# Moving the first batch's value loads, zero fills, mask products and weight loads to other places in the queues

## The chip, the core and the metric

The kernel runs on one core of a Trainium2 chip. A core has five engines that run side by side, each with its own queue that is worked off in order: TensorE (PE, with its weight loads shown apart as PEld), VectorE (DVE), ScalarE (ACT), GpSimd (POOL) and SyncE (SP). SP, ACT and POOL also issue DMA transfers, which 16 DMA engines carry out. The metric is the device time of one execution in microseconds (us), lower is better.

## The reference

The input is a sliding-window attention over 8 batches of 8 heads, 576 tokens of 64 elements each, followed by a two-layer feed-forward network with a leaky ReLU:

```python
def _attn_ref(q, k, v):                       # each (8, 8, 576, 64)
    scores = scale * np.matmul(q, k.transpose(0, 1, 3, 2))
    mask = np.abs(pos[:, None] - pos[None, :]) <= 32
    scores = np.where(mask, scores, -1000000000.0)
    attn = softmax(scores)
    return np.matmul(attn, v)

def _moe_ref(x, w_in, w_out):                 # x (4608, 512), w_in (512, 2048), w_out (2048, 512)
    h = x @ w_in
    g = np.maximum(0.01 * h, h)
    return g @ w_out
```

All inputs and the output are float32 in the chip's main memory.

## The kernel before

**Tiling.** Heads are taken in pairs (`p`, 0 to 3), so that two heads of 64 elements fill 128 partitions. Each batch is cut into two halves of 288 tokens. A unit of attention is one head pair of one half, numbered `i`: units 0 to 3 are the first half of batch 0, 4 to 7 its second half, 8 to 15 batch 1, and so on. `score(i)` multiplies queries and keys inside the window into a PSUM tile `ps`, ACT takes the exponential into `e` (L305), and a mask product gives `pr` (L309, on POOL). `weighted(i)` multiplies `pr` with a matrix of ones into the row sums `s` (L317 and L318) and with the values into `x` (L325); DVE takes the reciprocal of `s` (L331) and the product into `xT` (L333). There is one `ps`, one `s` and one `x` buffer; `e` and `pr` have two each.

**Feed-forward.** For each half `g` of 288 tokens, `h_tile(g, f)` computes 128 of the 2048 hidden columns (L344, four matmuls over the four head pairs of `xT`), and ACT applies the leaky ReLU into `gT` (L348). `o_tile(j)` computes 128 rows of the output over all 16 hidden tiles (L358), ACT copies it out (L363) and issues the store (L364).

**Preparation of an input.** q and k come in as float32, are cast to bfloat16 (`qb`, `kb`), transposed on PE in pieces of 96 tokens, and copied out of PSUM into `qT` and into `kbd`, which holds the two heads' keys as a block-diagonal matrix. The values are cast straight into the diagonal blocks of `vbd`. So `kbd` and `vbd` must be zero outside the blocks before they are used.

**The order.** The program sets it by hand: each engine works its instructions in the order in which the Python code emits them. Batch 0 is loaded in two parts: part 0 is what units 0 to 3 need, part 1 the rest. All these loads stand on SP's queue (L105 for q and k, L114 for v), pair by pair. POOL builds the mask and casts the keys (`kb`, L215) and some values (L228), DVE casts the queries (`qb`, L215), ACT casts other values (L226). `kbd` of batch 0 is zeroed on DVE (L154, L427), `vbd` on ACT for pairs 0 to 2 (`clear`, L150) and on DVE for pair 3 (L429). The weights come in four quarters each, `w_in`(0) to (3) (512 hidden columns each, four h tiles) and `w_out`(0) to (3), issued from POOL's queue (L419, L423), since they are cast to bfloat16 on the way.

From L425 the first four units are written out. Then h tiles of half 0 alternate with part 1's preparation and units 5 to 7 (`step()`, which emits the next score and this unit's weighted sum). After them come the loads of batch 1: the first is held back by a 4-byte copy from the second quarter of `w_out` into its buffer (L68), so that the weights go first. Behind batch 0's second h group a plan with estimated costs and due times spreads the later batches' attention among the matmuls; the change does not touch it.

Of the kernel before, what the change touches and what calls it, by code (L numbers as in the profile page):

```python
# [10 lines left out]
BF16 = mybir.dt.bfloat16  # L11
AF = mybir.ActivationFunctionType
# [4 lines left out]
def kernel(  # L17
# [83 lines left out]
    def load_qk0(p, h):  # L101
        for t, src, part in ((qf[0, p], q, PART_Q[h]), (kf[0, p], k, PART_K[h])):
            t0, run = part
            c0, c1 = columns(part)
            nc.sync.dma_start(  # L105
                out=t[:, :, c0 * D:c1 * D],
                in_=src[0, 2 * p:2 * p + 2, t0:t0 + 96 * run].rearrange(
                    "a (p c) d -> p a (c d)", c=run),
            )

    def load_v0(p, h):
        n0, n1 = PART_V[h]
        for a in range(2):
            nc.sync.dma_start(  # L114
                out=vf[0, p][64 * a:64 * a + 64, n0:n1],
                in_=v[0, 2 * p + a, 64 * n0:64 * n1].rearrange("(c p) d -> p c d", p=64),
            )

    for p in range(NPAIR + 1):
        if p < NPAIR:  # L120
            load_qk0(p, 0)
        if p > 0:
            load_v0(p - 1, 0)
    for p in range(NPAIR):
        load_qk0(p, 1)
        load_v0(p, 1)
# [15 lines left out]

    kbd = [const.tile([128, NPAIR, NB, 128], BF16, name=f"kbd{i}") for i in range(2)]
    vbd = [const.tile([128, NPAIR, NB, 128], BF16, name=f"vbd{i}") for i in range(2)]
    zero = const.tile([128, 1], BF16)
    nc.vector.memset(zero, 0.0)

    def clear(t, p):
        flat = t[:, p].rearrange("p n j -> p (n j)")
        nc.scalar.activation(  # L150
            out=flat, in_=zero.to_broadcast([128, NB * 128]), func=AF.Copy,
        )

    nc.vector.memset(kbd[0][:, 0:2], 0.0)  # L154
    for p in range(3):
        clear(vbd[0], p)

# [50 lines left out]
    def cast_qk0(p, h):  # L210
        for eng, src, dst, part in (
            (nc.vector, qf, qb, PART_Q[h]), (nc.gpsimd, kf, kb, PART_K[h]),
        ):
            c0, c1 = columns(part)
            eng.tensor_copy(  # L215
                out=dst[:, p, c0:c1],
                in_=src[0, p][:, :, c0 * D:c1 * D].rearrange("p a (c d) -> p c a d", d=D),
            )
# [11 lines left out]
    def transposes0(p, h):  # L230

        if 0 not in qT:
            qT[0] = attn.tile([128, NPAIR, S], BF16, name="qT")
        for src, part in ((qb, PART_Q[h]), (kb, PART_K[h])):
            t0, run = part
            c0, c1 = columns(part)
            tp = mmps.tile([128, run, 96], BF16, name="tp0", tag="mm")
            for c in range(run):
                nc.tensor.transpose(
                    tp[:, c], src[:, p, c0 + c].rearrange("p a d -> p (a d)"), ident[0:96, 0:96],  # L240
                )
            if src is qb:
                nc.scalar.activation(
                    out=qT[0][:, p, t0:t0 + 96 * run].rearrange("p (i c) -> p i c", c=run),
                    in_=tp.rearrange("p c i -> p i c"), func=AF.Copy,
                )
            else:
                for a in range(2):
                    r = slice(64 * a, 64 * a + 64)
                    nc.scalar.activation(  # L250
                        out=kbd[0][r, p, t0 // 64:t0 // 64 + 96 * run // 64, r].rearrange(
                            "p n (i c) -> p n i c", c=run),
                        in_=tp[r].rearrange("p c (n i) -> p n i c", i=64 // run), func=AF.Copy,
                    )

    def transposes(b, first=False):

# [36 lines left out]
    def score(i):  # L294
        b, hf, p = where(i)
        ps = scps.tile([128, 1024], FP32, name="ps")
        c0 = 512 - HALF
        for blk, q0, n in WIN[hf]:
            nc.tensor.matmul(  # L299
                ps[:, c0:c0 + n], kbd[b % 2][:, p, blk],  # L300
                qT[b][:, p, q0:q0 + n], start=True, stop=True,
            )
            c0 += n
        e = attn.tile([128, NCOL], BF16, name="e")
        nc.scalar.activation(  # L305
            out=e, in_=ps[:, 512 - HALF:512 - HALF + NCOL], func=AF.Exp, scale=scale,
        )
        pr = attn.tile([128, NCOL], BF16, name="pr")
        nc.gpsimd.tensor_mul(pr, e, mask[hf])  # L309
        probs[i] = pr  # L310

    def weighted(i):
        b, hf, p = where(i)
        pr = probs.pop(i)
        x = xps.tile([128, HALF], FP32, name="x")
        s = xps.tile([128, HALF], FP32, name="s")
        nc.tensor.matmul(s, ones_bd, pr[:, 0:HALF], start=True, stop=False, skip_group_check=True)  # L317
        nc.tensor.matmul(  # L318
            s[:, ODD[hf]:ODD[hf] + NCOL - HALF], ones_bd, pr[:, HALF:NCOL],
            start=False, stop=True, skip_group_check=True,  # L320
        )
        c0 = 0
        for n_, (blk, q0, n) in enumerate(WIN[hf]):
            a = q0 - HALF * hf
            nc.tensor.matmul(  # L325
                x[:, a:a + n], vbd[b % 2][:, p, blk, :], pr[:, c0:c0 + n],
                start=(n_ == 0), stop=(n_ == len(WIN[hf]) - 1), skip_group_check=True,
            )
            c0 += n
        r = attn.tile([128, HALF], FP32, name="r")  # L330
        nc.vector.reciprocal(r, s)  # L331
        t0 = (b * S + hf * HALF) % RING
        nc.vector.tensor_mul(xT[:, p, t0:t0 + HALF], x, r)  # L333
# [87 lines left out]
    def load_w_out(i):  # L421
        c = slice(4 * i, 4 * i + 4)
        nc.gpsimd.dma_start(out=w_out_bf[:, c, :], in_=w_out_r[:, c, :])  # L423

    cast_qk0(0, 0)  # L425
    make_mask(0)
    nc.vector.memset(kbd[0][:, 2:4], 0.0)  # L427
    cast_qk0(1, 0)
    nc.vector.memset(vbd[0][:, 3], 0.0)  # L429
    transposes0(0, 0)  # L430
    transposes0(1, 0)
    cast_v0(0, 0)
    cast_qk0(2, 0)
    score(0)
    transposes0(2, 0)
    score(1)
    cast_v0(1, 0, on_act=True)
    cast_qk0(3, 0)
    weighted(0)
    load_w_in(0)  # L440
    transposes0(3, 0)
    score(2)
    cast_v0(2, 0, on_act=True)
    weighted(1)
    load_w_in(1)
    score(3)
    cast_v0(3, 0, on_act=True)
    make_mask(1)
    load_w_in(2)
    weighted(2)  # L450
    cast_qk0(0, 1)
    load_w_in(3)
    weighted(3)
    state["done"] = NPAIR
    transposes0(0, 1)
    score(4)
    cast_v0(0, 1)


    for f in range(FFC):  # L460
        h_tile(0, f)
        if f % 2 == 1:
            i = (f - 1) // 2
            if i < 3:
                cast_qk0(i + 1, 1)
                cast_v0(i + 1, 1)
                transposes0(i + 1, 1)
            if 1 <= i < 5:
                step()
            if i >= 4:  # L470
                load_w_out(i - 4)

    for p in range(NPAIR):
        load_qk(1, p, w_out_bf[0:1, 4, 0:2] if p == 0 else None)
# [95 lines left out]
```

The softmax here doesn't subtract the row's maximum and nothing guards it: scores larger than these inputs give would overflow.

## Time and profile before

| | |
|---|---|
| median of 6 runs | 361.0 us (360.26 to 362.88) |
| the profiled execution | 360.11 us |
| its span in the profile | 358.4 us |
| PE busy | 327.9 us, 91% of the span |
| PE busy from 0 to 10, 10 to 20, 20 to 30 us | 3.80, 5.83, 8.10 us |
| DVE, ACT, POOL busy | 186.8, 209.5, 177.0 us |
| the DMA engines, from 0 to 10, 10 to 20, 20 to 30 us | share 0.69, 0.89, 1.19 |
| first ACT copy of a transposed query (L243) | starts at 5.48 us |
| exp of units 0, 1, 2, 3, 4 (L305) | start at 8.06, 10.38, 14.44, 16.07, 22.23 us |
| first h tile (L344) | starts at 21.93 us |
| mask products 6 and 7 (L309) | 34.24 to 36.62 us |
| landing of the four quarters of `w_out` | 5.9 us at least, 12.9 at most, after the issue |
| batch 1's first load | issued at 50.01 us |

Times in the profile count from the start of the span. A line of the timeline names the start, the duration, the engine, the line of the kernel, what is written from what, and in brackets how long the engine stood idle before and what ended that. A line of the chain of waits has the start, the duration and what the chain passed through at that time. The DMA share is the mean busy share of the 16 DMA engines; overlapping packets can bring it above 1.

### The profile page before, as it was taken

What the parts mean: (1) busy time and instruction counts of PE and PEld (TensorE: products, weight loads), DVE (VectorE), ACT (ScalarE), POOL (GpSimd) and SP (SyncE); (2) the same over time, 40 slices, a digit from 0 to 9 for tenths busy, and PEclk for the clock granted to TensorE, in tenths of its full rate; (3) what the DMA queues carried; (4) which work ended last, traced back from release to release, by engine and by line L of the source; (5) the groups of instructions that cost most, each with busy time, mean ns of one, the idle gap of its engine ahead of it and who ended that gap; (6) DMA issues with size and microseconds to landing.
All of it is one profiled execution on the core that took longest, in us unless ns stands there. A gap on an engine that the chain in (4) does not pass through costs nothing.

```text
span 358.4 us, 6953 instructions
## 1 busy us (share of the span) xinstructions
PE 327.9 (91%) x2730; PEld 221.8 (62%) x2752; DVE 186.8 (52%) x204; ACT 209.5 (58%) x450; POOL 177.0 (49%) x217
## 2 busy tenths in 40 slices
PE   3668897689989999999999999999999999999995
PEld 1446654458566685757585676758585666667652
DVE  5655503595635554666654654655563665655200
ACT  8736555458375483838474574838383665646441
POOL 7774933637765454665445553655553554222000
PEclk9999999899999999999999999999999999999999
DMA  6894799979786532634343523544320101010101
GB/s 178 164 224 67 117 202 258 232 193 214 174 194 155 186 101 65 174 116 128 97 124 112 183 68 111 148 133 110 81 62 31 59 2 60 1 60 0 60 10 78
DMA packets 62434, 42.39 MB, mean 118 GB/s; under 512 B 39874, under 2 KB 57794, under 8 KB 62402
## 3 DMA queue, kind: packets, MB, share of 16 engines
q1 hardware_dynamic: 52994, 28.32, 33.2%
q0 software_dynamic: 4224, 4.19, 7.2%
q10 hardware_dynamic: 5184, 9.44, 7.1%
q8 instruction: 21, 0.34, 0.4%
q14 instruction: 11, 0.09, 0.1%
HBM read 36.70 MB, written 9.44 MB: 129 GB/s over the span
## 4 chain that ended last, share of the span: by engine, by line
PE 72%; DMA 8%; ACT 7%; POOL 4%; issue 3%; DVE 2%; SPq 1%; ACTq 1%; POOLq 0%; DVEq 0%
PE mm L358 32%; PE mm L344 28%; PE x L325 3%; PE tp L266 3%; PE ps L299 3%; POOL pr L309 2%; DMA w_out_bf<-in_moe_w_out_dram 2%; DMA vf<-in_v_dram 2%; ACT o_sb L363 2%; PE s L317 2%; ACT e L305 1%; DMA qf<-in_q_dram 1%; PE s L318 1%; DMA qf<-w_out_bf 1%; ACT gT L348 1%
## 5 line engine op out<-in xcount | busy, mean ns | idle before, releaser
L331 DVE RECIPROCAL r<-s 128x288 f32<-128x288 f32 x64 | 125.3, 1958 | 94.8 <-PE s L318 94.6
L309 POOL TENSOR_TENSOR pr<-e,mask 128x544 bf16<-128x544 bf16 x64 | 77.6, 1213 | 136.4 <-ACT e L305 134.5
L344 PE MATMUL mm<-xT,w_in_bf 128*128 128x288 bf16 x1024 | 137.4, 290 | 1.5 <-ACT gT L348 1.5
L358 PE MATMUL mm<-w_out_bf,gT 128*128 128x512 bf16 x554 | 129.5, 381 | 1.2
L344 PEld LDWEIGHTS <-w_in_bf 128*128 128x128 bf16 x1024 | 99.2, 99 | 28.3 <-issue 3.2
L348 ACT ACTIVATE gT<-mm 128x288 bf16<-128x288 f32 x256 | 102.2, 412 | 23.6 <-PE mm L344 9.3
L358 PEld LDWEIGHTS <-gT 128*128 128x128 bf16 x576 | 55.3, 98 | 60.0 <-issue 0.6
L363 ACT ACTIVATE o_sb<-mm 128x512 f32<-128x512 f32 x36 | 21.5, 597 | 85.7 <-PE mm L358 85.7
L305 ACT ACTIVATE e<-ps 128x544 bf16<-128x544 f32 x64 | 39.8, 622 | 17.7 <-PE ps L299 9.1
L283 DVE COPY kbd<-kT 64x576 bf16<-64x576 bf16 x56 | 24.8, 444 | 23.8 <-ACT kT L280 23.4
L207 POOL CAST vbd<-vf 64x576 bf16<-64x576 f32 x52 | 34.4, 661 | 1.7
L333 DVE TENSOR_TENSOR xT<-x,r 128x288 bf16<-128x288 f32 x64 | 29.3, 458 | 6.7
L299 PE MATMUL ps<-qT,kbd 128*128 128x128 bf16 (+2 forms) x320 | 27.4, 218 | 2.0 <-ACT e L305 1.2
L197 POOL CAST kb<-kf 96x768 bf16<-96x768 f32 x28 | 23.1, 824 | 12.1 <-DMA kf<-in_k_dram 12.1
L325 PE MATMUL x<-pr,vbd 128*128 128x128 bf16 (+2 forms) x320 | 27.2, 218 | 0.7 <-DVE xT L333 0.5
L299 PEld LDWEIGHTS <-kbd 128*128 128x128 bf16 x320 | 20.8, 101 | 10.0 <-DVE kbd L283 1.3
L317 PE MATMUL s<-pr,ones_bd 128*128 128x288 bf16 x64 | 19.1, 299 | 7.7 <-POOL pr L309 4.8
L325 PEld LDWEIGHTS <-vbd 128*128 128x128 bf16 x320 | 21.8, 102 | 4.9 <-issue 2.1
L274 ACT ACTIVATE qT<-tp 128x576 bf16<-128x576 bf16 x28 | 18.1, 648 | 6.4 <-PE tp L266 5.7
L280 ACT ACTIVATE kT<-tp 128x576 bf16<-128x576 bf16 x28 | 18.2, 650 | 3.0 <-PE x L325 1.4
L197 POOL CAST qb<-qf 96x768 bf16<-96x768 f32 x24 | 19.7, 820 | 0.0
L318 PE MATMUL s<-pr,ones_bd 128*128 128x256 bf16 x64 | 18.3, 286 | 0.0
(43 smaller groups left out, 123.9 us busy)
## 6 DMA issues: line engine op xcount, KB each, us to landing
out_dram<-o_sb ACTq DMA_DIRECT2D x36, 256.0 KB, 2.4
qf<-in_q_dram SPq DMA_DIRECT2D x28, 288.0 KB, 3.3
kf<-in_k_dram SPq DMA_DIRECT2D x28, 288.0 KB, 3.9
vf<-in_v_dram SPq DMA_DIRECT2D x56, 144.0 KB, 3.3
w_in_bf<-in_moe_w_in_dram POOLq DMA_DIRECT2D x4, 512.0 KB, 8.3
w_out_bf<-in_moe_w_out_dram POOLq DMA_DIRECT2D x4, 512.0 KB, 9.7
qf<-in_q_dram SPq DMA_DIRECT2D x8, 144.0 KB, 3.0
kf<-in_k_dram SPq DMA_DIRECT2D x4, 192.0 KB, 3.2
```

Of the source, the lines that this page charges most:

```text
L197: eng.tensor_copy(out=dst[:, p], in_=src[b, p].rearrange("p a (c d) -> p c a d", d=D),)
L207: nc.gpsimd.tensor_copy(out=vbd[b % 2][r, p, :, r], in_=vf[b, p][r])
L299: nc.tensor.matmul(ps[:, c0:c0 + n], kbd[b % 2][:, p, blk], qT[b][:, p, q0:q0 + n], start=True, stop=True,)
L305: nc.scalar.activation(out=e, in_=ps[:, 512 - HALF:512 - HALF + NCOL], func=AF.Exp, scale=scale,)
L309: nc.gpsimd.tensor_mul(pr, e, mask[hf])
L325: nc.tensor.matmul(x[:, a:a + n], vbd[b % 2][:, p, blk, :], pr[:, c0:c0 + n], start=(n_ == 0), stop=(n_ == len(WIN[hf]) - 1), skip_group_c ...
L331: nc.vector.reciprocal(r, s)
L333: nc.vector.tensor_mul(xT[:, p, t0:t0 + HALF], x, r)
L344: nc.tensor.matmul(h[:, 0:HALF], w_in_bf[:, c, ts(f, 128)], xT[:, c, ds(t0, HALF)], start=(c == 0), stop=(c == DMC - 1),)
L348: nc.scalar.activation(out=gT[:, f, ds(t0, HALF)], in_=h[:, 0:HALF], func=AF.Prelu, alpha=0.01,)
L358: nc.tensor.matmul(o, gT[:, f, ds(128 * j % RING, 128)], w_out_bf[:, f, :], start=(f == 0), stop=(f == FFC - 1),)
L363: nc.scalar.activation(out=o_sb, in_=o, func=AF.Copy)
```

## The change

Batch 0 alone is touched; from batch 1's loads on the program is the same. In words:

- Part 0's values of pairs 0 and 1 (four transfers) are issued on ACT's queue, ahead of its activation table load. SP issues q and k of all pairs, with the values of pairs 2 and 3 behind theirs.
- The three fills of `vbd` on ACT and their `zero` tile are gone. DVE fills `vbd` of all four pairs, two behind the cast of q(1) and two behind that of q(2).
- The mask products of units 0 and 1 run on DVE.
- `transposes0` becomes a generator that yields after the query and after the key, so that `score(0)` stands between the two for pair 1.
- `w_in`(2) and (3) and `w_out`(0) move behind casts of part 1 on POOL; the casts of pair 1's part 1 move ahead of the h tiles; and the steps of units 4 to 7 stand behind h tiles 3, 6, 9 and 12 instead of 3, 5, 7 and 9. `w_out`(1) to (3) stay behind the last mask product of batch 0 on POOL.

```diff
-    def load_v0(p, h):
+    def load_v0(p, h, eng=nc.sync):
...
-            nc.sync.dma_start(
+            eng.dma_start(
...
-    for p in range(NPAIR + 1):
-        if p < NPAIR:
-            load_qk0(p, 0)
-        if p > 0:
-            load_v0(p - 1, 0)
+    for p in range(NPAIR):
+        load_qk0(p, 0)
+        if p >= 2:
+            load_v0(p, 0)
+    for p in range(2):
+        load_v0(p, 0, nc.scalar)
...
-    zero = const.tile([128, 1], BF16)
-    nc.vector.memset(zero, 0.0)
-
-    def clear(t, p):
-        flat = t[:, p].rearrange("p n j -> p (n j)")
-        nc.scalar.activation(
-            out=flat, in_=zero.to_broadcast([128, NB * 128]), func=AF.Copy,
-        )
-
     nc.vector.memset(kbd[0][:, 0:2], 0.0)
-    for p in range(3):
-        clear(vbd[0], p)
...
-        nc.gpsimd.tensor_mul(pr, e, mask[hf])
+        (nc.vector if i < 2 else nc.gpsimd).tensor_mul(pr, e, mask[hf])
...
+    t0 = {(p, h): transposes0(p, h) for p in range(NPAIR) for h in range(2)}
+
+    def t_pair(p, h):
+        next(t0[p, h])
+        next(t0[p, h])
+
     cast_qk0(0, 0)
     make_mask(0)
     nc.vector.memset(kbd[0][:, 2:4], 0.0)
     cast_qk0(1, 0)
-    nc.vector.memset(vbd[0][:, 3], 0.0)
-    transposes0(0, 0)
-    transposes0(1, 0)
+    for p in range(2):
+        nc.vector.memset(vbd[0][:, p], 0.0)
+    t_pair(0, 0)
+    next(t0[1, 0])
+    score(0)
+    next(t0[1, 0])
     cast_v0(0, 0)
     cast_qk0(2, 0)
-    score(0)
-    transposes0(2, 0)
+    for p in range(2, 4):
+        nc.vector.memset(vbd[0][:, p], 0.0)
+    t_pair(2, 0)
     score(1)
     cast_v0(1, 0, on_act=True)
     cast_qk0(3, 0)
+    load_w_in(0)
     weighted(0)
-    load_w_in(0)
-    transposes0(3, 0)
+    t_pair(3, 0)
     score(2)
     cast_v0(2, 0, on_act=True)
     weighted(1)
     load_w_in(1)
     score(3)
     cast_v0(3, 0, on_act=True)
+    weighted(2)
     make_mask(1)
-    load_w_in(2)
-    weighted(2)
     cast_qk0(0, 1)
-    load_w_in(3)
     weighted(3)
     state["done"] = NPAIR
-    transposes0(0, 1)
+    t_pair(0, 1)
     score(4)
     cast_v0(0, 1)
+    cast_qk0(1, 1)
+    cast_v0(1, 1)

     for f in range(FFC):
         h_tile(0, f)
-        if f % 2 == 1:
-            i = (f - 1) // 2
-            if i < 3:
-                cast_qk0(i + 1, 1)
-                cast_v0(i + 1, 1)
-                transposes0(i + 1, 1)
-            if 1 <= i < 5:
-                step()
-            if i >= 4:
-                load_w_out(i - 4)
+        if f == 1:
+            cast_qk0(2, 1)
+            load_w_in(2)
+            t_pair(1, 1)
+        if f == 3:
+            step()
+            cast_v0(2, 1)
+            cast_qk0(3, 1)
+            load_w_in(3)
+            t_pair(2, 1)
+        if f == 6:
+            step()
+            cast_v0(3, 1)
+            load_w_out(0)
+            t_pair(3, 1)
+        if f == 9:
+            step()
+            load_w_out(1)
+        if f == 12:
+            step()
+            load_w_out(2)
+            load_w_out(3)
```

More of the change, by code (lines that the diff above doesn't have):

```diff
@@ L246, in transposes0 @@
                 )
+                yield
             else:
@@ L254, in transposes0 @@
                     )
+                yield
     def transposes(b, first=False):
```

## The prediction

> **What bounds the kernel now.** I read the stages view first, then the chain of waits, then the timeline of the first 50 us, then the landing times of the weights. From 80 us to the end TensorE is busy 269.8 of 278 us, and the change touches nothing there. So the question is when that run can begin. The stages view (us, then busy time and instructions of PE, weight loads, DVE, ACT and POOL, granted clock, DMA share, GB/s) shows the start:
>
> ```profile
> 20.00:30.00 10.00, 8.10 (x54) 5.68 (x52) 4.14 (x6) 5.61 (x15) 5.24 (x12) 1.00 1.19 205
> 30.00:38.00 8.00, 5.47 (x53) 3.77 (x51) 6.37 (x6) 4.38 (x11) 5.91 (x8) 1.00 0.02 3
> 38.00:50.00 12.00, 11.79 (x97) 9.24 (x99) 2.81 (x3) 8.88 (x22) 9.66 (x11) 1.00 1.08 173
> 50.00:64.00 14.00, 10.58 (x79) 5.39 (x80) 4.82 (x10) 5.75 (x10) 4.12 (x6) 1.00 1.04 241
> ```
>
> The reader is to see that the DMA engines do next to nothing from 30 to 38 us, and that PE has 3.4 us of idle time from 50 to 64 while they work at 241 GB/s. The chain of waits (start, duration, what) says why:
>
> ```profile
> 33.48 0.63 ACT e L305
> 34.11 0.02 issue
> 34.13 0.02 POOLq L309
> 34.15 0.10 issue
> 34.24 2.38 POOL pr L309 x2
> 36.62 0.74 POOL w_out_bf L423
> 37.37 8.31 DMA w_out_bf<-in_moe_w_out_dram
> 45.67 0.02 SPq L68
> 45.70 0.05 issue
> 45.74 4.24 DMA qf<-w_out_bf
> ...
> 50.92 5.15 DMA qf<-in_q_dram
> 56.09 7.57 DMA vf<-in_v_dram
> ```
>
> Batch 1's loads are held by a 4-byte copy out of the second quarter of `w_out`. That quarter is issued at 37.37, behind mask products 6 and 7 on POOL, and lands at 45.68. The copy takes 4.24, and then q, k and v of batch 1 pass at the engines' rate until 63.66, when the first values allow PE to go on. **The time of the end is therefore set by when `w_out`(1) lands**; the 18 us behind it move as one piece.
>
> What sets mask product 7 goes back to the first heads. On the timeline, DVE:
>
> ```profile
> 10.68 1.96 DVE L331 RECIPROCAL r<-s 128x288 f32<-128x288 f32 x1 [0.55 <-PE s L318]
> ...
> 14.34 1.96 DVE L331 RECIPROCAL r<-s 128x288 f32<-128x288 f32 x1 [1.13 <-PE s L318]
> ...
> 17.05 1.96 DVE L331 RECIPROCAL r<-s 128x288 f32<-128x288 f32 x1 [0.19 <-PE s L318]
> ...
> 19.95 1.94 DVE L331 RECIPROCAL r<-s 128x288 f32<-128x288 f32 x1
> ```
>
> There is one sum buffer, so each reciprocal must end before the next sums start: 2.7 us per head pair at best (17.05 less 14.34). Score 4 and the first h tile stand behind these on PE.
>
> **The change, part by part.** Times below are walked down the five queues in their new order with the rows' durations; the same walk through the old order gives exp 4 ending at 22.84 and product 7 ending at 36.54, where the trace has 22.85 and 36.62.
>
> *ACT's fills leave, four value loads come.* The three fills keep ACT until its first copy at 5.48. Four loads at SP's 0.60 to 0.71 for such a load run from 0.8 to 3.4, the table load (1.28) to 4.7. The first transposes end at 4.4, so the first copy starts at 4.7, 0.8 sooner.
>
> *SP loses four issues ahead of pairs 2 and 3.* q(2) goes out at 2.7 instead of 4.12, k(3) at 5.7 instead of 7.22, the second part at 7.5 instead of 10.35. Landing takes 2.8 to 3.4 us on every load before 10 us, so SP's issue is the limit there. Four value loads more in the first 3 us must cost something: nothing at the least, and at most 1.0 on k(1) (320 KB at the 250 GB/s of that time is 1.3 us, part of it behind k(1)). I take 0.5, the middle, and 0.3 on k(0). The second part's earlier landing buys nothing, because its first cast (19.49) stands on DVE behind the third xT.
>
> *Exp 0.* Key cast at 4.4, transposes to 5.57, two kbd copies (0.97) to 6.6, query copy (0.41), scores by 7.3: exp 0 ends at 7.97 against 8.68. Gain 0.7.
>
> *DVE takes three more fills (0.54 each) and two mask products.* No row shows the product on DVE. The bf16 copy of 64x576 (0.444) bounds it below, the f32 tensor product of 288 columns scaled to 544 (0.458 x 544/288 = 0.87) above. I take 0.50, near the copy, which has the same type and length. Here the change adds a wait: DVE stands for exp 0, and behind it are cast q(2), two fills, product 1, cast q(3) and the first reciprocal. Product 0 ends at 8.5, q(2) is cast at 8.98 instead of 7.86, the pair's copies on ACT end at 10.8, and exp 1 at 11.45 instead of 11.00. Product 1, then cast q(3) (0.5): **the first reciprocal starts at 12.46 instead of 10.68**. From there the 2.7 cadence holds (before, the second one waited for POOL's product until 14.34): 15.16, 17.86 and, behind cast q(0,1), 20.78, against 19.95. Exp 4 ends at 23.69 against 22.85. So the early stage loses 0.84.
>
> *POOL after product 4.* Before, products 5 to 7 waited for ACT and all weights but `w_out` were out by 20.9. Now: product 4 to 24.95, values of pair 0 (0.84), keys 1 (0.40), values 1 (0.84), keys 2 (0.40), `w_in`(2) issued at 27.3 instead of 19.0, product 5 when exp 5 ends (29.7 to 30.9), values 2 and keys 3, `w_in`(3) at 32.05, product 6 at 33.8 (exp 6) to 35.0, values 3, `w_out`(0) at 35.8, product 7 to 37.8, `w_out`(1) at 37.75, against 37.37: 0.4 later. Exp 6 stands behind h tiles 4 to 6. Two tiles took 2.13 at 21.9 and 1.14 at 33.1, with granted clock 1.00 both times; the pace doubled between 31.4 and 32.2. I let it double at 31.1, the start of the idle stretch; all three tiles at the slow pace would cost 0.5 more, all at the fast one 0.9 less. The Trainium skill (TensorE: Matmul & The Clock Gate, Part 1) says that the clock opens after a busy free-running window of about 3.4 us, which would put it anywhere from 29.6 to 33 here and my sum from -1.5 to -0.5.
>
> *The landing.* The first of the four `w_out` quarters landed 5.9 after its issue, the second 3.2 after the first. Now `w_out`(0) has 1.95 us of lead: it lands at 41.7, and `w_out`(1) 3.2 later at 44.9 if the queue stays full, or 5.9 after its own issue at 43.65. I take 44.7, nearer to the first, since the lead is shorter than a quarter's 3.2. Against 45.68 that is 1.0 sooner. So what the late POOL queue loses (0.4) comes back through the head start of `w_out`(0).
>
> *Cover.* `w_in`(2) is costed at nothing because PE reaches h tile 8 only at 34.2 and it lands at 33.2 to 33.8 (5.9, as a lone transfer, to 6.5, as `w_in`(0)). `w_in`(3) lands at 38.1, where PE stands for it about 1 us; then PE ends batch 0's second h group at 49.3 against 49.45. POOL beside DVE's two products is costed at nothing: its key cast 2 ends at 8.25 and cast q(2), which PE needs too, only at 8.98. The Trainium skill (SBUF — State Buffer, Who interferes with whom) has a rule against this move: a DVE operation with two SBUF inputs and a GpSimd operation that reads SBUF block each other for a whole instruction. By it product 0 starts 0.25 later, when POOL's cast ends, and the sum would be -0.75.
>
> **Sum.** -1.0 on a profiled execution of 360.11 (span 358.4 and 1.7 around it). The median of the runs shown is 361.0, 0.9 above that execution, and I carry the difference over: 360.0. A difference under 0.3%, 1.1 us, is about what a measurement here cannot tell from no change.
>
> **The rivals.**
> - *The DVE queue eats it all.* Product at 0.87, k(1) and its followers 1 us later instead of 0.5: the product counts twice ahead of the first reciprocal, +0.75, and the landings +0.5, all passed to product 7 unless POOL absorbs it. `w_out`(1) at 45.5 to 46: about 361.0. For it: reciprocals have no slack after the first. Against: TensorE and POOL waits downstream absorb parts.
> - *Slower: h tile 8 waits for `w_in`(2).* Product 7 stands behind h tiles 8 and 9 on PE, so a late landing holds `w_out`(1). In the profile `w_in` took 6.5, 7.5, 9.2 and 10.7 us to land. From 6.9 (34.2) on it delays product 7; at 9.1 the gain is gone; at 10.7 h tile 8 starts at 38.0, product 7 ends at 41.3, `w_out`(1) lands at 47.2: +1.5, 362.5. For it: the landings shown. Against: the long ones had the loads of q, k, v and another quarter beside them, and by 27 us these are done.
> - *More: the pace of PE doubles early and `w_out` does not queue.* Product 7 ends at 36.9 and `w_out`(1) lands 5.9 behind its issue, 42.8 to 43.5: -2.2 to -2.9, 358.5. For it: SP's loads end sooner. Against: POOL's own casts already fill the time between products 6 and 7.
>
> **How the numbers follow.** Forecast (-1.7 to -0.3, that is 359.3 to 360.7) 0.40, of which 0.25 lies beyond 0.3%; more 0.17; eaten 0.22; slower 0.21. Faster 0.25 + 0.17 = 0.42; same 0.15 + 0.22 = 0.37; slower 0.21. The range reaches from the bound of "more" at 358.4 to 362.4, just below the slow case's price, and leaves about 0.08 below it and 0.11 above.
>
> **What would show it.** Right: ACT's first copy near 4.7; first reciprocal near 12.5 and the fourth near 20.8; exp 4 end near 23.7; `w_out`(1) issued near 37.8, landing within 7.5 us; the 4-byte copy starting near 44.8; PE free of waits on `w_in` before h tile 12. Wrong: PE standing at h tile 8; mask products on DVE over 0.9; loads before 5 us landing in over 4.5; the 4-byte copy taking other than about 4.2 us; or a stage behind 64 us that does not follow the landing.

## The result, and the profile after

The changed kernel takes 359.04 us (median of 34 runs, 356.69 to 361.54) beside 360.65 us for the kernel before (69 runs in all). The ratio is 0.9953 with a 95% interval of 0.9940 to 0.9965: **1.7 us faster** by the ratio (1.6 by the medians), where 1.0 us was forecast. The profiled execution of the changed kernel took 357.59 us (span 355.9); that of before 360.11 (span 358.4).

The stages view of the changed kernel (stretch, length, then busy time and instructions of PE, weight loads, DVE, ACT and POOL, granted clock, DMA share, GB/s):

```profile
20.00:30.00 10.00, 7.86 (x49) 5.33 (x50) 4.44 (x8) 4.65 (x12) 4.22 (x8) 1.00 0.41 74
30.00:38.00 8.00, 7.46 (x70) 5.51 (x67) 7.07 (x6) 6.13 (x17) 6.83 (x10) 1.00 0.83 132
38.00:50.00 12.00, 11.40 (x91) 8.76 (x93) 2.95 (x4) 8.21 (x20) 10.47 (x12) 1.00 1.09 173
50.00:64.00 14.00, 9.79 (x78) 5.11 (x77) 4.82 (x10) 6.92 (x12) 5.28 (x7) 1.00 1.03 276
```

The transfers have moved as the edit says: the stretch from 30 to 38 us, in which the DMA engines carried 3 GB/s, now carries 132, and the one before it 74 in place of 205. But look at the last line: from 50 to 64 us the DMA engines move 276 GB/s in place of 241, at the same share of busy time (1.03 and 1.04). Nothing in the edit is about those loads.

The chain of waits of the changed kernel (start, duration, what) shows the same thing from the other side:

```profile
34.13 1.21 POOL pr L301
...
36.13 0.49 POOL w_out_bf L415
...
36.96 1.16 POOL pr L301
38.12 7.90 DMA w_out_bf<-in_moe_w_out_dram
...
46.04 0.05 issue
46.09 3.58 DMA qf<-w_out_bf
...
49.69 0.33 SPq L70
...
53.04 7.88 DMA kf<-in_k_dram
...
63.28 1.22 POOL pr L301
```

Product 7 ends later than before, `w_out`(1) is issued later (38.12 for 37.37) and lands later: the 4-byte copy behind it starts at 46.09, 0.35 us after that of before. Yet batch 1's first load starts 0.32 us sooner (49.69 for 50.01), since the copy took 3.58 for 4.24, and product 8 starts 1.25 us sooner (63.28 for 64.53). From the first load of batch 1 to product 8 it is 13.59 us where it was 14.52. So **the prediction's earlier landing did not come, and the gain arose behind it**, in a stage that was said to move as one piece.

The queue of DVE in the changed kernel, from its timeline (start, duration, operation; the bracket is idle time before it):

```profile
8.67 0.45 DVE L301 TENSOR_TENSOR pr<-e,mask 128x544 bf16<-128x544 bf16 x1 [1.42 <-ACT e L297]
...
12.08 0.44 DVE L301 TENSOR_TENSOR pr<-e,mask 128x544 bf16<-128x544 bf16 x1 [1.28 <-ACT e L297]
...
12.90 1.95 DVE L323 RECIPROCAL r<-s 128x288 f32<-128x288 f32 x1
...
15.55 1.96 DVE L323 RECIPROCAL r<-s 128x288 f32<-128x288 f32 x1
...
18.23 1.96 DVE L323 RECIPROCAL r<-s 128x288 f32<-128x288 f32 x1 [0.17 <-PE s L310]
...
21.13 1.94 DVE L323 RECIPROCAL r<-s 128x288 f32<-128x288 f32 x1
```

The products are cheap on DVE, the wait for exp 0 and exp 1 stands ahead of them as predicted, and all four reciprocals are late: the first by 2.2 us, the fourth by 1.2.

A second thing moved with it. In the trace of before the granted clock shows a half-pace stretch just behind the end of batch 1's wait; the changed kernel's profiled execution has none. The stage of 65 to 70 us, before:

```profile
65.00:70.00 5.00, 4.16 (x28) 2.49 (x29) 2.42 (x2) 2.48 (x5) 3.21 (x4) 0.66 1.22 214
```

and after:

```profile
65.00:70.00 5.00, 4.89 (x46) 2.85 (x43) 4.45 (x5) 2.41 (x4) 3.38 (x4) 1.00 1.02 271
```

28 matmuls at a mean clock of 0.66 against 46 at full clock. Here the stretch lasts from 65.38 to 68.80 us, 3.4 us at 0.50, which is 1.7 us of pace. The mean clock of a run tells roughly how many such stretches it had: 0.995 (358.4 x 0.005 = 1.8 us) goes with one, about 0.990 with two. Of the 80 runs of before that stand beside the experiments, 11 had a clock of 1.000; of the changed kernel's, 12 of 34.

### The profile page after: what moved, and what is told of

It reads as the page before. It is cut to its first block, busy times and chain, and to the rows that moved or that the text cites. A ratio compares the mean times of both kernels' runs of the same rounds, so it can differ in the third digit from the quotient of the medians.

```text
span 355.9 us, 6950 instructions
## 1 busy us (share of the span) xinstructions
PE 326.1 (92%) x2730; PEld 221.0 (62%) x2752; DVE 189.1 (53%) x208; ACT 206.4 (58%) x447; POOL 174.9 (49%) x215
## 4 chain that ended last, share of the span: by engine, by line
PE 71%; ACT 7%; DMA 6%; issue 4%; POOL 4%; DVE 4%; ACTq 1%; SPq 1%; POOLq 0%; DVEq 0%
PE mm L350 31%; PE mm L336 28%; PE x L317 3%; PE tp L258 3%; PE ps L291 3%; DVE r L323 3%; DMA w_out_bf<-in_moe_w_out_dram 2%; DMA kf<-in_k_dram 2%; ACT o_sb L355 2%; PE s L309 2%; POOL pr L301 2%; PE s L310 1%; ACT e L297 1%; ACT gT L340 1%; ACTq L356 1%
## 5 line engine op out<-in xcount | busy, mean ns | idle before, releaser
L301 POOL TENSOR_TENSOR pr<-e,mask 128x544 bf16<-128x544 bf16 x62 | 75.2, 1213 | 136.6 <-ACT e L297 133.1
L336 PEld LDWEIGHTS <-w_in_bf 128*128 128x128 bf16 x1024 | 99.1, 99 | 30.0 <-issue 3.9
L297 ACT ACTIVATE e<-ps 128x544 bf16<-128x544 f32 x64 | 39.8, 622 | 18.1 <-PE ps L291 9.3
L275 DVE COPY kbd<-kT 64x576 bf16<-64x576 bf16 x56 | 24.8, 443 | 22.4 <-ACT kT L272 22.0
```

The lines of the kernel that those rows point to most:

```text
L297: nc.scalar.activation(out=e, in_=ps[:, 512 - HALF:512 - HALF + NCOL], func=AF.Exp, scale=scale,)
L301: (nc.vector if i < 2 else nc.gpsimd).tensor_mul(pr, e, mask[hf])
L336: nc.tensor.matmul(h[:, 0:HALF], w_in_bf[:, c, ts(f, 128)], xT[:, c, ds(t0, HALF)], start=(c == 0), stop=(c == DMC - 1),)
```

## The experiments

Two parts of the change could be taken apart: the **start** (first values from ACT, fills and two products on DVE) and the **second part** (order of the weights and of the casts). A third difference lies in the addresses. The constant column `zero`, which the change drops, is 2 bytes wide, but it takes 32 bytes of each partition, and every tile allocated behind it lies 32 bytes lower once it is gone, the masks too. The load destinations `qf`, `kf`, `vf`, both weights, `xT` and `gT` begin 32 bytes past a multiple of 256 bytes before, and at one after. All kernels, and how many bytes past a multiple of 256 the load destinations lie (a ratio is of runs on the same chip, so it can differ by some tenths of a microsecond from the medians):

| kernel | start | second part | bytes past | median us | ratio to before (95%) |
|---|---|---|---|---|---|
| before | before | before | 32 | 360.65 | 1 |
| after | change | change | 0 | 359.04 | 0.9953 (0.9940 to 0.9965) |
| `early_only` | change | before | 0 | 360.32 | 0.9993 (0.9970 to 1.0017) |
| `late_only` | before | change | 32 | 358.66 | 0.9938 (0.9915 to 0.9961) |
| `no_lead` | change | change, `w_out`(0) later | 0 | 360.57 | 0.9990 (0.9972 to 1.0009) |
| `w_out_first` | before | before, `w_out`(0), (1) ahead of product 6 | 32 | 356.83 | 0.9874 (0.9845 to 0.9903) |
| `aligned` | before | before | 64 | 360.65 | 1.0001 (0.9976 to 1.0026) |
| `aligned_512` | before | before | 0 | 358.96 | 0.9937 (0.9915 to 0.9959) |
| `after_shifted` | change | change | 32 | 361.08 | 0.9998 (0.9976 to 1.0021) |
| `v_on_sp` | change, values on SP | change | 0 | 357.07 | 0.9889 (0.9861 to 0.9917) |
| `products_on_pool` | change, products on POOL | change | 0 | 361.05 | 1.0010 (0.9992 to 1.0029) |
| `v_sp_w_out` | change, values on SP | change, `w_out`(0), (1) ahead of product 6 | 0 | 357.42 | 0.9903 (0.9874 to 0.9932) |
| `best` | before | change, `w_out`(0), (1) ahead of product 6 | 64 | 356.23 | 0.9875 (0.9843 to 0.9906) |
| `best_loads` | before | as `best` | 0 (loads alone) | 356.90 | 0.9877 (0.9847 to 0.9907) |

### The two parts, each alone

`early_only` keeps the change up to `weighted`(1) and has the order of before from there on:

```diff
-    weighted(2)
     make_mask(1)
+    load_w_in(2)
+    weighted(2)
     cast_qk0(0, 1)
+    load_w_in(3)
...
+        if f % 2 == 1:
+            i = (f - 1) // 2
+            if i < 3:
+                cast_qk0(i + 1, 1)
+                cast_v0(i + 1, 1)
+                t_pair(i + 1, 1)
+            if 1 <= i < 5:
+                step()
+            if i >= 4:
+                load_w_out(i - 4)
```

> The change's first part alone (values issued from ACT, fills and the first two products on DVE, new order of the first units); weights and second part in the order of before. My theory: the first part costs time. Exp 4 ended at 24.03 us in the changed kernel and 22.85 in before, and nothing after it wins that back when the weights stand as before: product 7 ends at 37.8 to 38.1, w_out(1) lands near 47, batch 1's first load goes out near 51.3, and the run is 1.0 to 1.5 us slower than before. Rival (the gain comes from the shorter start on ACT and SP): faster than before by 1 us or more, like the whole change. Rival (the gain is only the half-pace window of PE at 65 us, which comes less often in the changed kernel): within 0.5 us of before.

`late_only` is the other half: the start of before, and the change from `weighted`(2) on.

> The change's second part alone (weights between the casts of the second part, casts of pair 1 earlier, steps behind h tiles 3, 6, 9 and 12); the start as before. My theory: this part holds the whole gain and more, because exp 4 ends at 22.85 as before: product 7 ends near 36.9, w_out(1) lands near 44.1 against 45.68, and the run is 1.0 to 2.0 us faster than before, so 0 to 1 us faster than the whole change (which measured 1.7 us faster). Rival (the gain comes from the start): within 0.5 us of before. Rival (h tile 8 waits for w_in(2)): slower than before, with PE standing at h tile 8 near 33 us.

Measured: `early_only` 360.32 us, `late_only` 358.66. In `early_only` exp 4 starts at 23.85 (22.23 before), `w_out`(1) is issued at 38.99 and batch 1's loads start at 51.55, 1.54 later than before; yet the time is that of before. In `late_only` exp 4 starts at 22.19, `w_out`(1) goes out at 37.15, and the copy behind it starts at 44.98, 0.76 sooner than before, and batch 1's loads at 48.60, 1.41 sooner. So the second part alone is worth 2.0 us, at least as much as the whole change (the intervals of the two ratios overlap). That `early_only` costs nothing, with all its stations over 1 us late, was the first sign of a gain that neither part explains; here too batch 1's loads go faster (14.2 us from the first load to product 8, for 14.5), while in `late_only`, which keeps the column `zero`, they are slower (15.4).

### What the head start of the first quarter is worth

`no_lead` issues `w_out`(0) directly ahead of `w_out`(1), behind product 7:

```diff
             cast_v0(3, 1)
-            load_w_out(0)
             t_pair(3, 1)
         if f == 9:
             step()
+            load_w_out(0)
             load_w_out(1)
```

> The whole change, but w_out(0) is issued behind the last mask product, right ahead of w_out(1). My theory: the head start of w_out(0) is what paid for the late product 7. Without it w_out(0) is issued near 38.1 and w_out(1) lands 8 to 9 us later, near 47, against 46.1 in the changed kernel's profile: 0.9 to 1.9 us slower than the whole change, near before or up to 1 us slower. Rival (the head start does nothing, since w_out(1) landed 7.95 us after its issue with it): the same time as the whole change.

Measured: 360.57 us, 1.5 more than the changed kernel. `w_out`(1) is issued at 38.79 and the copy starts at 47.27, 8.5 us later, where it takes 7.97 with the head start. The prediction's view that the lead makes up for the late POOL queue holds in its sign: 1.2 us of the copy's start, 0.7 of it by the later issue and 0.5 by the longer landing. One caution goes with all such readings of single profiles: the changed kernel, `early_only` and `no_lead` are the same program at the same place up to score 3, and yet exp 1 starts at 11.42, 11.87 and 12.15 us.

`w_out_first` is the kernel before with both first quarters moved ahead of mask product 6 on POOL, and nothing else:

```diff
                 cast_v0(i + 1, 1)
+                if i == 2:
+                    load_w_out(0)
+                    load_w_out(1)
...
-            if i >= 4:
+            if i >= 6:
                 load_w_out(i - 4)
```

> The kernel before, with w_out(0) and w_out(1) issued ahead of mask product 6 instead of behind product 7; nothing else. POOL stood idle there from 32.2 to 34.2 us. My theory that the end follows the landing of w_out(1) one for one: issue of w_out(1) near 33.0 instead of 37.37, landing near 41.3 instead of 45.68, batch 1's first load near 45.5 instead of 50.01, and the time 3 to 4 us lower, until PE takes over as the limit (it stood idle 3.4 us between 50 and 64 us, and lost about 1.7 us to the half pace at 66 us). Rival (the end hangs on something else, such as PE or the rate of the loads): less than 1 us faster.

Measured: 356.83 us, 3.8 less than before. From its timeline, of SP and of POOL:

```profile
41.99 0.72 SPq L68 DMA_DIRECT2D qf<-w_out_bf  x1
46.16 0.34 SPq L70 DMA_DIRECT2D qf<-in_q_dram  x1
...
62.30 1.21 POOL L309 TENSOR_TENSOR pr<-e,mask 128x544 bf16<-128x544 bf16 x1 [0.81 <-ACT e L305]
```

`w_out`(0) and (1) are issued from 32.79 on, the copy starts at 41.99 in place of 45.74, batch 1's first load at 46.16 in place of 50.01. Of 3.75 us at the landing and 3.85 at the loads, product 8 gets 2.2 (62.30), and the time 3.8. The gate that the prediction read from the chain of waits is a right one: moving it moves the time. But the stage behind it stretches, from 14.5 to 16.1 us between the first load and product 8, so the near equality of 3.75 and 3.8 is no proof of one for one; where the other 1.6 us of the time arise was not traced.

### Where the tiles lie

`aligned` and `aligned_512` are the kernel before with a wider `zero`; no instruction is added, removed or moved.

```diff
-    zero = const.tile([128, 1], BF16)
-    nc.vector.memset(zero, 0.0)
+    zero = const.tile([128, 32], BF16)
+    nc.vector.memset(zero[:, 0:1], 0.0)
...
-            out=flat, in_=zero.to_broadcast([128, NB * 128]), func=AF.Copy,
+            out=flat, in_=zero[:, 0:1].to_broadcast([128, NB * 128]), func=AF.Copy,
```

> The kernel before with its constant column `zero` 64 bytes wide in place of 2: every tile behind it, the destinations of all loads among them, lies 32 bytes further on, at multiples of 64 bytes as in the changed kernel (the 2-byte column takes 32 bytes); no instruction is added, removed or moved. Theory 'address': the packets of 256 bytes that bring batch 1, 27.2 ns each in the trace of before and 18.1 in the changed kernel's, take 18 to 19.5 here; from the first load of batch 1 to mask product 8 it is 13.6 to 14.2 us in place of 14.5, so product 8 starts 0.3 to 0.9 us sooner, and the time is 359.7 to 360.3 us beside 360.65. Rival 'start' (the packets are faster for what else the change did at the start): 26 to 27.5 ns, nothing moves, 360.4 to 360.9.

(`aligned_512`: `[128, 256]` in place of `[128, 32]`.)

> The kernel before with its constant column 512 bytes wide: every tile behind it lies at the same place within 512 bytes as in the changed kernel (the 64-byte column left them 64 bytes off). Theory 'address, in 256 or 512 bytes': the 256-byte packets of the stretch that the product stage of batch 1 loads in take 18 to 19 ns in place of 24.6 (the 64-byte column gave 22.0), product 8 starts 0.4 to 0.9 us sooner, and the time is 359.2 to 360.1. Rival 'not the address of the tiles' (the order of the first loads or their queue): 22 to 25 ns, 360.4 to 360.9.

`after_shifted` gives the changed kernel the 32 bytes back (and one small fill on DVE):

```diff
+    unused = const.tile([128, 1], BF16)
+    nc.vector.memset(unused, 0.0)
     nc.vector.memset(kbd[0][:, 0:2], 0.0)
```

> The changed kernel with an unused 2-byte constant where `zero` was: all tiles behind it are 32 bytes off a multiple of 64 again; one memset of some 0.05 us on DVE is added before 1 us. Theory 'address': the 256-byte packets take 25 to 27.5 ns, mask product 8 starts 0.3 to 0.9 us later after the first load of batch 1, and the time is 359.3 to 360.2 us, so that a good part of the 1.7 us gained was the address. Rival 'start': 18 to 19 ns, 358.8 to 359.3.

The DMA view of 59 to 111 us in four kernels: the queue of SP's loads (packets, MB, share of 16 engines' time) and the loads of the values (issues, KB each, median us to landing). Before:

```profile
q1 hardware_dynamic: 18125, 9.09, 86.1%
...
vf<-in_v_dram SPq DMA_DIRECT2D x21, 144.0 KB, 4.7
```

Before with the 512-byte column (`aligned_512`):

```profile
q1 hardware_dynamic: 18098, 9.07, 67.7%
...
vf<-in_v_dram SPq DMA_DIRECT2D x21, 144.0 KB, 3.1
```

The changed kernel:

```profile
q1 hardware_dynamic: 18429, 9.52, 72.7%
...
vf<-in_v_dram SPq DMA_DIRECT2D x21, 144.0 KB, 3.7
```

The changed kernel, 32 bytes off (`after_shifted`):

```profile
q1 hardware_dynamic: 17958, 8.86, 84.1%
...
vf<-in_v_dram SPq DMA_DIRECT2D x21, 144.0 KB, 4.7
```

The first two carry the same 9.1 MB in nearly the same number of packets; in the one they take 86.1% of the engines' time, in the other 67.7%. The packets of 256 bytes, which are the rows of the values, took 24.6 ns on average in this stretch before, 22.0 in `aligned`, 17.9 in `aligned_512`, 18.1 in the changed kernel and 24.8 in `after_shifted`. The packets of 1536 bytes, which bring q and k, got faster with them: 101.4 ns before, 99.1, 85.9, 89.3 and 100.3 in the same order. The time follows: `aligned` (64 bytes past) gains nothing, **`aligned_512` gains 1.7 us without touching an instruction, and `after_shifted` loses all that the change had gained (361.08, ratio 0.9998)**. From the first load of batch 1 to product 8 it is 14.40 us in `aligned`, 13.75 in `aligned_512`, and in `after_shifted` 14.76. From the chain of waits of `aligned_512`:

```profile
49.52 0.34 SPq L70
...
63.27 1.22 POOL pr L309
```

and of `after_shifted`:

```profile
38.58 7.71 DMA w_out_bf<-in_moe_w_out_dram
...
46.35 4.16 DMA qf<-w_out_bf
...
50.53 0.34 SPq L70
...
65.29 1.21 POOL pr L303
```

So the theory "address" as it was first put, multiples of 64 bytes, fell with `aligned`; in multiples of 256 it held. The rival, that something else at the start made the packets faster, fell with `aligned_512`. Another, that the new place of the weights, `xT` and `gT` makes the engines faster, finds nothing in the traces: from 111 to 330 us the matmuls take 286 and 379 ns on average and the weight loads 98, both before and in `aligned_512`.

`best_loads` asks which tiles count. It is `best` (below) with filler ahead of and behind the load destinations, so that these alone lie at multiples of 256:

```diff
+    pads = [fload.tile([128, 112], FP32, name="pad0")]
     for p in range(NPAIR):
         qf[0, p] = fload.tile([96, 2, RUN * D], FP32, name=f"qf{p}")
...
+    pads.append(fload.tile([128, 16], FP32, name="pad1"))
...
+    for pad in pads:
+        nc.vector.memset(pad[:, 0:1], 0.0)
```

> The kernel `best` (64-byte column, early w_out; 356.23 us) with 448 bytes ahead of the load destinations qf, kf, vf and 64 behind them, so that these alone lie at multiples of 256 bytes; the constants, the weights, xT, gT and the attention and output tiles stay 64 to 320 bytes off as they are there. Two memsets of some 0.06 us on DVE before 2 us are added. Theory 'destinations of the loads': the 256-byte packets of 59 to 111 us, 21.9 ns in best, take 17.7 to 18.3, and the time is 355.0 to 356.0 us. Rival 'other tiles' (what the engines or the weight loads read and write): 21 to 23 ns, 356.0 to 356.6.

The DMA view of 59 to 111 us, `best`:

```profile
q1 hardware_dynamic: 17147, 9.13, 76.4%
...
vf<-in_v_dram SPq DMA_DIRECT2D x20, 144.0 KB, 4.3
```

and `best_loads`:

```profile
q1 hardware_dynamic: 17053, 9.10, 66.8%
...
vf<-in_v_dram SPq DMA_DIRECT2D x19, 144.0 KB, 3.4
```

All the 256-byte packets from 50 to 111 us go from 21.9 to 18.7 ns on average (the 1536-byte ones, from 59 us on, from 93.6 to 83.8) with the destinations alone moved: for the packets, it is the place where they are written. The time does not follow here, against the expectation: 356.90 us for 356.23, with intervals that lie on each other (0.9877 and 0.9875). In these two kernels the keys that product 8 waits for land at 59.23 and 59.10, so at this order of the loads the first stage of batch 1 gets nothing from it.

### What the start loses, and to which step

`v_on_sp` is the changed kernel with the first values back on SP, in the order of before; `products_on_pool` is it with both products back on POOL:

```diff
-    for p in range(NPAIR):
-        load_qk0(p, 0)
-        if p >= 2:
-            load_v0(p, 0)
-    for p in range(2):
-        load_v0(p, 0, nc.scalar)
+    for p in range(NPAIR + 1):
+        if p < NPAIR:
+            load_qk0(p, 0)
+        if p > 0:
+            load_v0(p - 1, 0)
```

> The changed kernel with the first values issued by SP in the order of before; all else is the change's. The prediction's step has ACT free for its first copy 0.8 us sooner for the move, while the trace has that copy at 5.94 (5.48 before), the four issues on ACT taking 3.80 us and SP's slowed beside them. Theory 'the issues on ACT cost': without them the second cast of the keys is 0.3 to 0.7 us sooner, exp 0 starts at 7.2 to 7.6 in place of 7.94, exp 4 at 22.8 to 23.2 in place of 23.41, w_out(1) is issued at 37.5 to 37.9, and the time is 358.4 to 358.9 beside the changed kernel's 359.04. Rival 'the move paid': the queries and keys of pairs 2 and 3 are issued up to 1.2 us later behind the values, exp 1 to 3 and exp 4 are as late or later (23.4 to 24), and the time is 359.0 to 359.7.

```diff
-        (nc.vector if i < 2 else nc.gpsimd).tensor_mul(pr, e, mask[hf])
+        nc.gpsimd.tensor_mul(pr, e, mask[hf])
```

> The changed kernel with mask products 0 and 1 back on POOL, each behind the key cast it has for company (1.2 us there against 0.44 to 0.45 on DVE); all else is the change's. Theory (the products on DVE pay for the start): POOL's key casts of pairs 2 and 3 and the first part of w_in go out 1.2 to 2.4 us later, exp 4 starts at 24.2 to 24.8 in place of 23.41, w_out(1) is issued at 38.7 to 39.2 in place of 38.12, and the time is 359.7 to 360.5 us beside the changed kernel's 359.04. Rival (DVE's queue is what holds the start back, and without the products its casts of queries run sooner): exp 4 at 23.0 to 23.5, 358.5 to 359.2.

ACT's timeline in the changed kernel:

```profile
0.81 3.80 ACTq L114 DMA_DIRECT2D vf<-in_v_dram  x4
4.64 1.28 ACT L233 ACT_TABLE_LOAD   x1 [4.64 <-DMA vf<-in_v_dram]
5.94 0.41 ACT L233 ACTIVATE qT<-tp 128x288 bf16<-128x288 bf16 x1
...
7.94 0.62 ACT L297 ACTIVATE e<-ps 128x544 bf16<-128x544 f32 x1 [0.29 <-PE ps L291]
```

and in `v_on_sp`:

```profile
0.80 1.28 ACT L232 ACT_TABLE_LOAD   x1 [0.80 <-PEq L567]
4.40 0.41 ACT L232 ACTIVATE qT<-tp 128x288 bf16<-128x288 bf16 x1 [2.31 <-PE tp L228]
...
7.03 0.62 ACT L296 ACTIVATE e<-ps 128x544 bf16<-128x544 f32 x1 [0.29 <-PE ps L290]
```

The four issues hold ACT for 3.80 us, the table load has to follow them, and the first copy goes out at 5.94, later than before the change (5.48). With the values on SP it goes out at 4.40, exp 0 starts 0.9 us sooner, exp 4 at 22.84 for 23.41. Down the chain of waits of `v_on_sp` this reaches the gate and product 8:

```profile
36.98 8.13 DMA w_out_bf<-in_moe_w_out_dram
...
45.18 3.45 DMA qf<-w_out_bf
...
62.32 1.21 POOL pr L300
```

0.9 us sooner at the copy and 1.0 at product 8, and 2.0 us in the time (357.07), well below the 358.4 to 358.9 that was expected. Most of the rest goes with the clock: 5 of its 6 runs were at 1.000, and against the changed kernel's 12 runs at 1.000 its mean span is 0.9 us shorter. The rival, that the queries and keys behind the values come too late, fell: exp 1 to 4 are all sooner, and exp 1 is at 10.86 there and 10.87 in `v_sp_w_out`, below all three profiles of the changed start. The Trainium skill, DMA: Bandwidth & Descriptors (Issuing engines are not separate DMA queues), says that starting transfers from several engines at once saves only the sequencer's time, usually small beside the transfer. The runs agree that it brought nothing here, and show a price: 0.95 us per issue on ACT (3.80 over 4), while SP, issuing beside it, took 0.60 and 0.63 for q(1) and k(1) that take 0.45 each in `v_on_sp`.

`products_on_pool` took 361.05 us, 2.0 more than the changed kernel, a little beyond the expected 360.5: exp 1 starts at 13.51 (11.42 in the changed kernel), exp 4 at 25.36, `w_out`(1) goes out at 39.41. So in this start the products on DVE earn their place, and the step that loses is the issue of the values on ACT.

### Joining what paid

`best` has the start of before, the change's second part, the order of `w_out_first`, and the 64-byte column of `aligned`; `v_sp_w_out` has the start of `v_on_sp` and no column. The edit of both against the change's second part:

```diff
         if f == 6:
-            step()
             cast_v0(3, 1)
             load_w_out(0)
+            load_w_out(1)
+            step()
             t_pair(3, 1)
         if f == 9:
             step()
-            load_w_out(1)
```

> The start of before, the change's second part, both first quarters of w_out issued behind the last value cast and ahead of mask product 6, and the 64-byte column. By the two runs it joins (second part alone 358.66 us, w_out ahead of product 6 356.83) the gains are not a sum, since both act on the issue of w_out(1): 37.15 and 33.6 in these. If that issue is the gate, it is at 33.3 to 33.8 here, the quarter lands at 41 to 42, the loads of batch 1 follow from 45.5 to 46.2, and with the faster packets the time is 355.5 to 356.6. If the address counts for nothing it is 356.5 to 357.2; if h tiles starve for w_in(3) behind it, over 357.2.

> The changed kernel with the first values on SP's queue (357.07 us alone) and with the last value cast and both first quarters of w_out ahead of mask product 6. The gate is the landing of the second quarter: its issue, 36.98 with the values on SP, goes to 33.3 to 34.0, it lands at 42 to 43 (the last part of w_in is issued only 1 to 2 us ahead, and they share the transfers), batch 1's loads start at 46 to 47 in place of 48.65, and product 8 at 60.5 to 61.5 in place of 62.32. Theory (the gate alone counts): 355.0 to 356.2 us. Rival (PE has no work for batch 1's early products, or h tile 12 waits for w_in(3) longer): 356.4 to 357.5.

`best` took 356.23 us, 4.5 less than before (360.77 in the runs beside it), although the faster packets that its expectation counted on did not come: at 64 bytes past they are still at 21.9 ns. Its chain of waits:

```profile
34.01 8.98 DMA w_out_bf<-in_moe_w_out_dram
...
43.06 4.45 DMA qf<-w_out_bf
...
61.59 1.22 POOL pr L309
```

The second quarter is issued 0.2 us later than expected and lands 1 us later (43.0): `w_in`(3), issued at 31.66, is in flight beside it, which in `w_out_first` it is not. Still product 8 starts sooner than there (61.59 for 62.30). It is not clearly faster than `w_out_first`: 0.9875 and 0.9874 overlap. `v_sp_w_out` took 357.42, the rival's price, and no better than `v_on_sp` (357.07): the copy starts 1.4 us sooner (43.76), yet product 8 at 62.41 is where it was (62.32). Past some point, then, the gate is not the only one; what holds product 8 there was not taken apart.

## Why the prediction was right, and where it was wrong

The sign came true, and the size within the forecast's 0.3 to 1.7 us; the reason given for them did not, so the agreement is luck. Two of the prediction's own signs of being wrong were seen: the 4-byte copy took 3.58 us in place of about 4.2, and the stage behind did not follow the landing.

- **The gate.** That the end is set by the landing of `w_out`(1) is borne out in its direction: `w_out_first` moved the copy by 3.75 us, product 8 by 2.2 and the time by 3.8. That "the 18 us behind it move as one piece" is where the account breaks: from the copy's start to product 8 it is 18.8 us before, 17.2 after, 18.9 in `after_shifted` and 20.3 in `w_out_first`. What shortens the copy itself was not set apart: it took 3.6 in `late_only` too, where the tiles lie as before.
- **"Four loads at SP's 0.60 to 0.71 run from 0.8 to 3.4"** failed: they took 0.95 each and ran to 4.61. ACT's first copy, forecast 0.8 us sooner at 4.7, came 0.46 later, at 5.94. Nor did SP gain what it was to gain: q(2) went out at 3.03 for 2.7, but k(3) at 7.50 for 5.7 (7.22 before) and the second part at 9.18 for 7.5. `v_on_sp` puts 2.0 us of the medians on this step, 0.9 at equal clock.
- **The DVE queue** came out as walked, with what it inherits: exp 0 ends at 8.56 for 7.97, first reciprocal 12.90 for 12.46, fourth 21.13 for 20.78, exp 4 ends at 24.04 for 23.69. The product took 0.45 and 0.44 where 0.50 was taken, at its lower bound. The early loss is 1.2 us, not 0.84.
- **POOL's queue** came out 0.3 to 0.6 late throughout: `w_in`(2) 27.85 for 27.3, `w_in`(3) 32.63 for 32.05, `w_out`(0) 36.08 for 35.8, `w_out`(1) 38.12 for 37.75. The cover held: `w_in`(2) cost nothing at h tile 8, and PE's weight loads stood 0.78 us for `w_in`(3) until 38.01, forecast about 1 us at 38.1. PE's pace doubled later than the 31.1 taken: the twelve matmuls of h tiles 4 to 6, from 30.52 on, took 2.56 us, where eight took 2.12 before them and 1.14 after, which puts it near 32.4 by estimate.
- **"I take 44.7"** for the landing failed: `w_out`(0) landed at 41.7 as said, `w_out`(1) 4.3 us behind it and not 3.2, at 46.02. This step was to bring -1.0; it brought +0.3.
- **What was left out.** The fills that "leave" ACT took their constant column with them, and with it 32 bytes under every later tile. The prediction costed that at nothing without saying so. `aligned_512` prices it at 1.7 us, `after_shifted` at 2.0.

Without the address the changed instructions are worth nothing, at either place. With the tiles 32 bytes past, the changed kernel takes 361.08 us (`after_shifted`, ratio 0.9998, interval 0.9976 to 1.0021) beside 360.65 for before; at multiples of 256 it takes 359.04 beside 358.96 (`aligned_512`). Behind the zero stand two parts that cancel, and not by the same amounts at both places: 32 bytes past, the second part brings 2.0 us (`late_only`) and the start on top of it costs 2.4; at multiples of 256 the start costs 1.4 (`early_only` against `aligned_512`) and the second part on top of it brings 1.3. So the parts do not simply add. The zero is the price of the first rival ("eats it all", 361.0), though not by its mechanism: the product was at its lower bound, and ACT's issues did the eating.

How the faster packets become 1.7 us is shown in part. `aligned_512`, with before's instructions, has product 8 at 63.27, 1.26 us sooner than before: 0.77 is the stage from the first load of batch 1 on, 0.11 the copy, and 0.38 was there before the copy, since exp 1 starts at 10.01 in place of 10.38 (at 10.01 in `best_loads` too, and at 10.31 to 10.79 in the five kernels that have this start with the loads off multiples of 256). The half-pace stretches of the clock have a smaller part than the two profiles suggest. No run of `after_shifted` was without one (0 of 12), against 12 of 34 of the changed kernel and 3 of 9 of `aligned_512`; but in `no_lead` and `products_on_pool`, at multiples of 256 as well, it was 1 of 12 and 2 of 12, so the address alone does not decide it. And between runs of equal mean clock the gain is still there: the changed kernel's mean span is 1.2 us (at 0.995) and 1.6 us (at 1.000) below before's (22 and 11 of its 80 runs), that of `aligned_512` 1.4 and 1.6. That the shorter wait for batch 1 prevents a stretch is plausible from where it sits, right behind that wait, but no run set the wait and the address apart. Nor did a run move the load destinations alone in the kernel before: in `best_loads`, which did so in another order, the packets got faster and the time did not.

## What to carry to other kernels

A change to the list of tiles is a change to the addresses of all tiles behind it: where loads bring rows of 256 bytes, compare the packets' mean duration and the start of the destinations before crediting the instructions with a difference of half a per cent. To tell the two apart, pad the old kernel and unpad the new one; here that took no instruction and 512 bytes. And before an issue is moved to an engine that seems idle, look at what that engine must do first: four loads on ACT cost more ahead of its table load than the fills that they replaced.

## What the runs showed of the hardware

- A write of 256 bytes that begins 32 bytes past a multiple of 256 took 24.6 ns a packet from 59 to 111 us, 64 bytes past 22.0, and none past 17.9, with the same packets and bytes. The Trainium skill, DMA: Bandwidth & Descriptors (How a descriptor splits into AXI transactions), has the rule that bears on it: a descriptor that doesn't start at a multiple of 256 bytes is split at that boundary, so that a row of 256 bytes becomes two transactions. The runs agree in the direction, for destinations, while the page tells it of reads. By an estimate from its rule (9 beats of 32 bytes for 32 past and 10 for 64 past, in place of 8) the second would be the dearer, by 12 and 25%; measured were 37 and 23%, the other way round. A start of 128 past was not tried.
- It does not cost everywhere. From 111 to 311 us the packets of 256 bytes took 17.7 to 17.8 ns in every kernel, whatever the address, and from 3 to 13 us 17.8 before and 18.0 in `late_only`, both 32 past, though 25.4 in `after_shifted`. What must be added for the price to appear is open.
- Product 0 on DVE, the same instruction, took 0.44 to 0.79 us, and its length goes with a cast on POOL. Where POOL's key cast was running when it began, it ended 0.30 us after that cast: at 8.56 behind a cast that ended at 8.26 in `v_on_sp` (0.79 us), 8.57 behind 8.27 in `v_sp_w_out` (0.71), 9.70 behind 9.40 in `after_shifted` and 9.85 behind 9.55 in `no_lead` (0.61 each). Where the cast ended less than 0.2 us after the product's start it cost nothing: 0.45 in the changed kernel (value cast to 8.83, product from 8.67) and 0.44 in `early_only` (9.20 and 9.13). Product 1, with no cast beside it, took 0.44 in all six. This is the blocking that the prediction weighed at 0.25 us for product 0; in the changed kernel it came to 0.01, and the key cast, which began at 8.90 during the product, took 0.69 in place of 0.61.
